# Attention and gated feed-forward in one kernel: PE transposes for the last 128 tokens of each chunk, pads of the second batch zeroed ahead of its DMA transposes, global rows doubled ahead

## The chip, the cores and the metric

One core of one Trainium2 chip runs the whole kernel. The metric is the device time of one execution in microseconds (us), lower is better. Before the change it is 449.09 us, the median of three runs (448.82 to 450.19).

The engines named below are PE (TensorE, matmuls; its weight loads are PEld), DVE (VectorE), ACT (ScalarE), POOL (GpSimd, which here also issues the loads) and SP (SyncE, which issues the DMA transposes and the stores). Each works through its own list of instructions in order, and semaphores hold one engine until another is done.

## What is computed

Attention with a window of 32 tokens and 8 global tokens over 8 batches x 8 heads x 576 tokens x 64 features, and behind it a gated feed-forward layer over all 4608 tokens (512 features, 1536 hidden):

```python
def _attn_ref(q, k, v, global_idx):
    scores = scale * np.matmul(q, k.transpose(0, 1, 3, 2))
    mask = np.abs(pos[:, None] - pos[None, :]) <= window
    mask = mask | is_global[:, None] | is_global[None, :]
    scores = np.where(mask, scores, -1000000000.0)
    scores = scores - np.max(scores, axis=-1, keepdims=True)
    attn = np.exp(scores)
    attn = attn / (np.sum(attn, axis=-1, keepdims=True) + 1e-09)
    return np.matmul(attn, v)

def _moe_ref(x, w_gate, w_val, w_out, w_res):
    g = x @ w_gate
    gelu = 0.5 * g * (1.0 + erf(g * inv_sqrt2))
    ffn_out = gelu * (x @ w_val) @ w_out
    res_gate = 1.0 / (1.0 + np.exp(-(x @ w_res)))
    return x + res_gate * ffn_out
```

x is the output of the attention, the heads of a token side by side. Matmuls run in bf16 with f32 sums.

## The kernel before, in words

**Chunks and batches.** The 4608 tokens are nine chunks of 512 (four tiles t = 0 to 3 of 128 tokens). A chunk is eight windows of 64 tokens, and a batch is nine windows, so chunk c uses batches c - 1 and c. The main loop (L491) runs over the chunks. While chunk c goes through the feed-forward layer, batch b = c + 1 is got ready and the attention of chunk c + 1 is computed, in between.

**First half of a chunk, ffn_in (L398).** Twelve rounds j, each of four matmuls into g_ps, four into v_ps, a Gelu on ACT (gsb) and a product on DVE (ht, L410). g_ps and v_ps take banks from psm, a pool of four PSUM banks that the other feed-forward results use too; ht gives v_ps's bank back. A second pool, pss (two banks, tag "sc"), holds the scores. Into these rounds the code puts the preparation of batch b: at the chunk's head turn_qk(b) (L295), ten DMA transposes issued by SP that write q and k of the batch with features on the partitions (qt, kt), and load_v(b); at j = 8 the shift of v, the load of the batch after it on POOL's queue, and prep_qz; at j = 11 the scores of the global tokens (sg, ss).

**Second half, ffn_out (L412).** Sixteen slots: for each tile a gate (r_ps, four matmuls) and three thirds of f_ps (twelve matmuls), with prb on DVE, ob on POOL and a store issued by SP at the end of the tile. Beside them stand the attention of the next chunk: scores in slots 0 to 7, values(t) in slot 5 + 2t (L351; its results are divided by DVE into xtok, L384), and turn_x(t) in slot 7 + 2t (L387), ahead of the slot's own work. turn_x writes xt, the chunk with features on the partitions, as ffn_in needs it. In chunk 0 it does so with four PE transposes into PSUM and a copy on ACT; in all later chunks with one DMA transpose that SP issues (L390). The last one, t = 3, stands in slot 13, ahead of the last twelve f_ps matmuls; the next chunk's first g_ps needs all four.

**Chunk 0 and batch 1.** The pads beside the data are written once for each of the two buffers. For batch 1 this stands in chunk 0: zero_qk(1) (L154, the halves of qz that stay zero and the pads of kt) behind round j = 0, zero_rest(1) (L160, ones and zeros in ve, pads of gt and ptg) behind j = 1, both on DVE. Ahead of the loop the loads of batch 1 (q, k, then v at L471) and of the weights (wr_t, wo_t) are put on POOL's queue, and behind them the gathers of the global rows of batches 2 to 7 (kgf, qgf, vgf, L191). turn_qk(1) stands at the head of chunk 0, ahead of zero_qk(1).

**Global rows.** spread_qk (L238) brings the gathered global rows of k and q into kgz and qgz: DVE doubles them in bf16 (kgd, qgd, L241), PE transposes them (tg, L245), DVE copies k's part and ACT q's (L250). It runs for the first pair of batches ahead of the loop (L457) and for the other three pairs in chunk 1 behind j = 6 (L512).

Of the kernel before, what the change touches and what calls it, by code (L numbers as in the profile page):

```python
# [9 lines left out]
BF16 = mybir.dt.bfloat16  # L10
# [6 lines left out]
def view(t, p0, pn, off, dims):  # L17

    step = t.ap[0][0]
    return bass.AP(tensor=t.tensor, offset=t.offset + p0 * step + off, ap=[[step, pn]] + dims)  # L20
# [3 lines left out]
def kernel(  # L24
# [12 lines left out]
    nc = tc.nc  # L37
    B, H, S, D = q.shape
# [14 lines left out]
    NKT = DM // 128  # L53
# [5 lines left out]
    pss = ctx.enter_context(tc.tile_pool(name="pss", bufs=2, space=bass.MemoryType.PSUM))  # L59
# [33 lines left out]
    def load_v(b):  # L93
        t = ve[b % 2]
        for c in range(5):
            p0, p1 = (32, 128) if c == 0 else (0, 96) if c == 4 else (0, 128)
            s0 = 128 * c - 32
            nc.gpsimd.dma_start(t[p0:p1, c, :, 0:D],  # L98
                                v[b].rearrange("h s d -> s h d")[s0 + p0:s0 + p1])
# [45 lines left out]
    def zero_wide(t, p0, pn, off, dims):  # L145

        w = [[st // 2, n] for st, n in dims[:-1]] + [[1, dims[-1][1] // 2]]
        b = t.bitcast(F32)
        nc.vector.memset(view(b, p0, pn, off // 2, w), 0.0)
# [4 lines left out]
    def zero_qk(i):  # L154
        for u in range(2):
            zero_wide(qz[i], 64 - 64 * u, 64, u * S, [[2 * S, NP], [1, S]])
        zero_wide(kt[i], 0, 128, 0, [[S + 64, NP], [1, 32]])
        zero_wide(kt[i], 0, 128, 32 + S, [[S + 64, NP], [1, 32]])
# [28 lines left out]
    gath = {what: const.tile([128, B // 2, D], F32, name=f"{what}gf", tag=f"{what}gf") for what in "kqv"}  # L187
# [41 lines left out]
    def hot_rows(i):  # L229
        r0 = 64 - 64 * (i % 2)  # L230
        nc.scalar.copy(gt[i][r0:r0 + 64, 64:64 + S], hot[r0:r0 + 64, :])


    twice = {what: const.tile([128, B // 2, 2, D], BF16, name=f"{what}gd", tag=f"{what}gd") for what in "kq"}
    vgb = const.tile([128, B // 2, VG], BF16, name="vgb", tag="vgb")
    nc.vector.memset(vgb[:, :, D:VG], 1.0)

    def spread_qk(n0, n1):  # L238
        nn = n1 - n0
        for what, big, pstep in (("k", kgz, 144), ("q", qgz, 16)):  # L240
            nc.vector.tensor_copy(twice[what][:, n0:n1, :, :],  # L241
                                  view(gath[what], 0, 128, n0 * D, [[D, nn], [0, 2], [1, D]]))
            tg = pss.tile([128, nn, 128], BF16, name="tg", tag="sc")
            for n in range(nn):
                nc.tensor.transpose(tg[:, n, :], twice[what][:, n0 + n, :, :].rearrange("p a d -> p (a d)"), ident)  # L245
            width = big.shape[2] * big.shape[3]
            for e in range(2):
                shift = 64 * e if what == "k" else 0
                for u in range(2):
                    (nc.scalar.copy if what == "q" else nc.vector.tensor_copy)(  # L250
                        view(big, 64 * u, 64, (2 * n0 + e) * width + shift + 8 * u,
                             [[2 * width, nn], [pstep, NP], [1, NG]]),
                        view(tg, 64 * u, 64, 64 * e + 8 * u, [[128, nn], [16, NP], [1, NG]]))
# [12 lines left out]
    def bank(shape, name, dt=F32):  # L266

        ring["n"] += 1
        if ring["n"] % 3 == 0:
            return pss.tile(shape, dt, name=name, tag="sc")  # L270
        return psm.tile(shape, dt, name=name, tag="mm")
# [23 lines left out]
    def turn_qk(b):  # L295
        for src, dst, c0 in ((q_st, qt[b % 2], 0), (k_st, kt[b % 2], 32)):
            for r in range(NQT):
                n = min(128, S - 128 * r)
                nc.sync.dma_start(dst[:, :, c0 + 128 * r:c0 + 128 * r + n], src[0:n, r, :], transpose=True)

    def prep_qz(b, p0, p1):
        for u in range(2):
            nc.vector.tensor_copy(qz[b % 2][64 * u:64 * u + 64, p0:p1, u, :],
                                  qt[b % 2][64 * u:64 * u + 64, p0:p1, :])
# [81 lines left out]

    def turn_x(c, t):  # L387
        mine = xt[c % 2][:, :, 128 * t:128 * t + 128]
        if c:
            nc.sync.dma_start(mine, xtok[c % 2][:, t, :], transpose=True)  # L390
            return
        tx = bank([128, NKT, 128], "tx", BF16)
        for kk in range(NKT):
            nc.tensor.transpose(tx[:, kk, :], xtok[c % 2][:, t, 128 * kk:128 * kk + 128], ident)
        nc.scalar.copy(mine, tx)


    def ffn_in(c, j):  # L398
# [45 lines left out]
    for p in range(NP + 1):  # L444
# [7 lines left out]
        if p:  # L452
            for what in "qk":
                turn_pair(p - 1, what, cast[what][1 if p < NP else 0])
            prep_qz(0, p - 1, p)
    hot_rows(0)
    spread_qk(0, 1)  # L457
    nc.vector.scalar_tensor_tensor(maskg, far, 1024.5, nong, ALU.is_gt, ALU.mult)
    shift_v(0)
# [31 lines left out]
    for c in range(NCH):  # L491
        b = c + 1
        if b < B:
            turn_qk(b)
            if b > 1:
                load_v(b)
        held = None
        for j in range(NFF):
            ffn_in(c, j)
            if b < B:  # L500
                if c == 0:
                    if j == 0:
                        zero_qk(1)
                    elif j == 1:
                        zero_rest(1, nc.vector)
                        hot_rows(1)
                    elif j == 2:
                        zero_globals(2, B)
                        spread_vg(1, nc.vector)
                if c == 1:  # L510
                    if j == 6:
                        spread_qk(1, B // 2)  # L512
                        spread_v(1, B // 2)
                    elif j == 8:
                        for n in range(2, B):
                            spread_vg(n, nc.gpsimd)
                if j == 8:
                    shift_v(b)
                    if b + 1 < B:
                        load_qk(b + 1)  # L520
                    prep_qz(b, 0, NP)
                if j == 11:
                    held = global_scores(b)
        slots = {n: [] for n in range(16)}
        if c + 1 < NCH:
            if held is not None:
                slots[0].append(lambda: global_exp(b, *held))
                slots[4].append(lambda: global_rows(b))
            for n in range(8):
                slots[n].append(lambda n=n: scores(c + 1, n // 4, n % 4))  # L530
            for t in range(4):
                slots[5 + 2 * t].append(lambda t=t: values(c + 1, t))
                slots[7 + 2 * t].insert(0, lambda t=t: turn_x(c + 1, t))
        work_f = [w for t in range(4) for w in ffn_out(c, t)]
        for n in range(16):
            for w in slots[n]:
                w()
            work_f[n]()
# [30 lines left out]
```

## Time and profile before

| | |
|---|---|
| median of three runs | 449.09 us (448.82, 449.09, 450.19) |
| the profiled execution | 448.51 us |
| its span, first to last instruction | 446.8 us |
| mean granted clock of PE | 0.975 |
| busy: PE / DVE / ACT / POOL | 87% / 46% / 38% / 37% |
| DMA moved | 47.60 MB, 107 GB/s over the span |
| xt by DMA transpose | 32 issues, median 2.4 us from issue to landing |
| qt and kt by DMA transpose | 35 each, median 7.1 and 5.2 us |

The profile is of one execution, with times from the span's start. A row of a timeline has start, duration, engine, line, operation, output <- input, shapes and a count; in square brackets stands the idle time of the engine just before it and what ended it. Equal instructions that follow each other make one row, whose duration runs from the first start to the last end. A row of the waits has the waiting engine and line, what it waited for, the total in us, how often, and the longest. A row of groups has the busy time, the mean of one in ns, and the idle time before. Some matmul records can be missing, so a group of four is sometimes shown as three.

### The profile page before, as it was taken

The page shows a single profiled execution, that of the slowest core. Times are in us where ns is not written, and L with a number is a line of the kernel's source. Part 1 is how long each engine was busy: PE and PEld are TensorE (multiplying, and loading weights), DVE is VectorE, ACT ScalarE, POOL GpSimd, SP SyncE. Part 2 cuts the span into 40 slices and gives each one's busy share as a digit, 9 for nine tenths or more (in the row PEclk, how much of TensorE's full clock was granted, in tenths as well). Part 3 has the DMA queues.
Part 4 walks back from the last instruction along what each step waited for, and adds up shares of the span by engine and source line. Part 5 has one row for each costly group of instructions (what it writes and reads, how often), then busy time and mean ns, then how long its engine had stood idle before and what let it go on. Part 6 is the DMA issues. An engine that isn't in the chain of part 4 may idle for free.

```text
span 446.8 us, 7136 instructions
## 1 busy us (share of the span) xinstructions
PE 387.6 (87%) x2718; PEld 207.3 (46%) x2762; DVE 204.5 (46%) x388; ACT 169.5 (38%) x274; POOL 167.2 (37%) x194
## 2 busy tenths in 40 slices
PE   2487049989799899989989998999899989998995
PEld 1373015644365346534644564456445644463442
DVE  6672055634555355435543553356344633462321
ACT  5364014523263236323623452345235423533320
POOL 6577346542672561257125613551420120022012
PEclk9999569999899999999999999999999999999999
DMA  7999997939393998399639973993592230022001
GB/s 173 168 168 156 167 209 108 126 94 152 70 114 76 138 175 84 83 129 182 62 96 126 172 77 82 151 173 50 100 148 67 37 106 2 0 73 70 0 23 72
DMA packets 168994, 47.60 MB, mean 107 GB/s; under 512 B 156480, under 2 KB 163136, under 8 KB 168960
## 3 DMA queue, kind: packets, MB, share of 16 engines
q0 software_dynamic: 108784, 18.62, 60.8%
q1 hardware_dynamic: 60176, 28.53, 32.2%
q8 instruction: 21, 0.34, 0.3%
q14 instruction: 13, 0.11, 0.1%
HBM read 39.19 MB, written 9.44 MB: 109 GB/s over the span
## 4 chain that ended last, share of the span: by engine, by line
PE 54%; issue 21%; DMA 13%; POOL 5%; DVE 3%; ACT 1%; SPq 1%; POOLq 0%; DVEq 0%
PE g_ps L402 15%; PE v_ps L406 14%; PE f_ps L429 11%; DMA wo_t<-in_moe_w_out_dram 4%; PE r_ps L419 4%; POOL ob L435 3%; DMA xt<-xtok 3%; DMA qt<-q_st 3%; PE sc L344 2%; PE nd L370 2%; DMA wo_t<-in_k_dram 2%; PE sg L310 2%; PE sn L332 1%; PE nd L364 1%; POOL k_st L90 1%
## 5 line engine op out<-in xcount | busy, mean ns | idle before, releaser
L406 PE MATMUL v_ps<-xt,wv_t 128*128 128x512 bf16 x417 | 110.3, 383 | 19.7 <-DVE ht L410 19.3
L410 DVE SCALAR_TENSOR_TENSOR ht<-gsb,v_ps 128x512 bf16<-128x512 bf16 x108 | 73.9, 687 | 112.7 <-PE v_ps L406 105.1
L409 ACT ACTIVATE gsb<-g_ps 128x512 bf16<-128x512 f32 x108 | 64.5, 597 | 158.3 <-PE g_ps L402 136.9
L402 PE MATMUL g_ps<-xt,wg_t 128*128 128x512 bf16 x429 | 112.1, 383 | 14.0 <-DMA xt<-xtok 12.9
L435 POOL TENSOR_TENSOR ob<-prb,xtok 128x512 f32<-128x512 f32 x36 | 41.9, 1163 | 204.0 <-DVE prb L433 201.7
L429 PE MATMUL f_ps<-wo_t,ht 128*128 128x512 bf16 x414 | 102.1, 379 | 0.9
L406 PEld LDWEIGHTS <-wv_t 128*128 128x128 bf16 x432 | 42.6, 99 | 71.5 <-issue 21.7
L402 PEld LDWEIGHTS <-wg_t 128*128 128x128 bf16 x432 | 42.0, 99 | 67.2 <-issue 13.3
L429 PEld LDWEIGHTS <-ht 128*128 128x128 bf16 x432 | 38.8, 98 | 35.9
L347 ACT ACTIVATE pt<-sc 128x512 bf16<-128x512 f32 x72 | 41.8, 598 | 28.4 <-PE sc L344 28.3
L422 ACT ACTIVATE rsb<-r_ps 128x512 bf16<-128x512 f32 x36 | 21.5, 596 | 61.8 <-PE r_ps L419 48.3
L349 DVE TENSOR_TENSOR pt<-pt,maskw 128x512 bf16<-128x512 bf16 x72 | 31.3, 437 | 27.1 <-ACT pt L347 25.6
L433 DVE SCALAR_TENSOR_TENSOR prb<-rsb,f_ps 128x512 f32<-128x512 bf16 x36 | 24.6, 684 | 33.4 <-PE f_ps L429 33.2
L90 POOL DMA_DIRECT2D q_st<-in_q_dram x35 | 30.0, 874 | 23.4 <-DMA qt<-q_st 23.4
L419 PE MATMUL r_ps<-wr_t,xt 128*128 128x512 bf16 x136 | 36.4, 379 | 0.4
L98 POOL DMA_DIRECT2D ve<-in_v_dram x40 | 34.3, 870 | 1.5 <-DMA k_st<-in_k_dram 1.5
L90 POOL DMA_DIRECT2D k_st<-in_k_dram x35 | 31.0, 912 | 6.6 <-DMA kt<-k_st 4.1
L344 PE MATMUL sc<-qz,kt 128*128 128x128 bf16 x288 | 27.8, 224 | 0.1
L344 PEld LDWEIGHTS <-kt 128*128 128x128 bf16 x288 | 21.8, 100 | 12.0
L384 DVE TENSOR_TENSOR xtok<-nd,rden 128x512 bf16<-128x512 f32 x34 | 23.5, 692 | 1.2
L370 PEld LDWEIGHTS <-pt 128*128 128x128 bf16 x576 | 22.3, 97 | 1.0
L370 PE MATMUL nd<-ve,pt 128*128 128x65 bf16 x320 | 22.3, 193 | 0.0
(103 smaller groups left out, 249.3 us busy)
## 6 DMA issues: line engine op xcount, KB each, us to landing
out_dram<-ob SPq DMA_DIRECT2D x36, 256.0 KB, 2.2
vo<-ve SPq DMA_DIRECT2D x16, 260.0 KB, 6.0
q_st<-in_q_dram POOLq DMA_DIRECT2D x28, 128.0 KB, 5.2
k_st<-in_k_dram POOLq DMA_DIRECT2D x28, 128.0 KB, 4.7
ve<-in_v_dram POOLq DMA_DIRECT2D x24, 128.0 KB, 5.5
ve<-in_v_dram POOLq DMA_DIRECT2D x16, 96.0 KB, 9.8
wg_t<-in_moe_w_gate_dram POOLq DMA_DIRECT2D x3, 512.0 KB, 6.1
wv_t<-in_moe_w_val_dram POOLq DMA_DIRECT2D x3, 512.0 KB
```

The lines of the kernel that those rows point to most:

```text
L90: nc.gpsimd.dma_start(dst[0:n, r, :].rearrange("p (h d) -> p h d", d=D), src[b].rearrange("h s d -> s h d")[128 * r:128 * r + n])
L98: nc.gpsimd.dma_start(t[p0:p1, c, :, 0:D], v[b].rearrange("h s d -> s h d")[s0 + p0:s0 + p1])
L344: nc.tensor.matmul(sc[:, n, :, :], kt[b % 2][:, p, 64 * i:64 * i + 128], qz[b % 2][:, p, :, 64 * i:64 * i + 64], start=True, stop=True)
L347: nc.scalar.activation(mine, sc, ACTF.Exp, bias=0.0, scale=SCALE)
L370: nc.tensor.matmul(nds[h // 4][:, VG * (h % 4):VG * (h % 4) + VG], view(pt, 0, 128, c0, [[1, 128]]), vw, start=False, stop=(h % 4 == 3 and ...
L402: nc.tensor.matmul(g_ps, wg_t[:, kk, 128 * j:128 * j + 128], x[:, kk, :], start=(kk == 0), stop=(kk == NKT - 1))
L406: nc.tensor.matmul(v_ps, wv_t[:, kk, 128 * j:128 * j + 128], x[:, kk, :], start=(kk == 0), stop=(kk == NKT - 1))
L409: nc.scalar.activation(gsb, g_ps, ACTF.Gelu, bias=0.0, scale=1.0)
L410: nc.vector.scalar_tensor_tensor(ht[:, j, :], gsb, 0.5, v_ps, ALU.mult, ALU.mult)
L419: nc.tensor.matmul(r_ps, xt[c % 2][:, kk, 128 * t:128 * t + 128], wr_t[:, kk, :], start=(kk == 0), stop=(kk == NKT - 1))
L429: nc.tensor.matmul(held["f"], ht[:, j, 128 * t:128 * t + 128], wo_t[:, j, :], start=(j == 0), stop=(j == NFF - 1))
L435: nc.gpsimd.tensor_tensor(ob, prb, xtok[c % 2][:, t, :], ALU.add)
```

## The change

turn_x for t = 3 of chunks 1 to 8 goes back to four PE transposes, into a bank of pss, with the copy to xt on DVE; t = 0 to 2 stay DMA transposes. zero_qk(1) stands at the head of chunk 0, ahead of turn_qk(1). The doubling is taken out of spread_qk into a function of its own: for the first pair both casts stand ahead of the transposes, for the other three pairs they stand in chunk 1 behind j = 3. zero_rest(1) keeps its place.

```diff
+    def double_qk(n0, n1):
+        for what in "kq":
+            nc.vector.tensor_copy(twice[what][:, n0:n1, :, :],
+                                  view(gath[what], 0, 128, n0 * D, [[D, n1 - n0], [0, 2], [1, D]]))
+
     def spread_qk(n0, n1):
         nn = n1 - n0
         for what, big, pstep in (("k", kgz, 144), ("q", qgz, 16)):
-            nc.vector.tensor_copy(twice[what][:, n0:n1, :, :],
-                                  view(gath[what], 0, 128, n0 * D, [[D, nn], [0, 2], [1, D]]))
             tg = pss.tile([128, nn, 128], BF16, name="tg", tag="sc")
...
     def turn_x(c, t):
         mine = xt[c % 2][:, :, 128 * t:128 * t + 128]
-        if c:
+        if c and t < 3:
             nc.sync.dma_start(mine, xtok[c % 2][:, t, :], transpose=True)
             return
-        tx = bank([128, NKT, 128], "tx", BF16)
+        tx = pss.tile([128, NKT, 128], BF16, name="tx", tag="sc") if c else bank([128, NKT, 128], "tx", BF16)
         for kk in range(NKT):
             nc.tensor.transpose(tx[:, kk, :], xtok[c % 2][:, t, 128 * kk:128 * kk + 128], ident)
-        nc.scalar.copy(mine, tx)
+        (nc.vector.tensor_copy if c else nc.scalar.copy)(mine, tx)
...
     hot_rows(0)
+    double_qk(0, 1)
     spread_qk(0, 1)
...
         if b < B:
+            if c == 0:
+                zero_qk(1)
             turn_qk(b)
...
                 if c == 0:
-                    if j == 0:
-                        zero_qk(1)
-                    elif j == 1:
+                    if j == 1:
                         zero_rest(1, nc.vector)
                         hot_rows(1)
...
                 if c == 1:
-                    if j == 6:
+                    if j == 3:
+                        double_qk(1, B // 2)
+                    elif j == 6:
                         spread_qk(1, B // 2)
```

The places where instructions move, in the order of the built program (line numbers behind the first edit are three higher in the changed kernel).

DVE at the start of chunk 0, before (qz_77 and kt_79 are batch 1's buffers, ve_81 its v):

```order
L410 SCALAR_TENSOR_TENSOR ht<-gsb,v_ps 128x512
L149 MEMSET qz_77 64x4x288 x2
L149 MEMSET kt_79 128x4x16 x2
L410 SCALAR_TENSOR_TENSOR ht<-gsb,v_ps 128x512
L161 MEMSET ve_81 128x40
L162 MEMSET ve_81 32x520
```

The same place in the changed kernel:

```order
L149 MEMSET qz_77 64x4x288 x2
L149 MEMSET kt_79 128x4x16 x2
L413 SCALAR_TENSOR_TENSOR ht<-gsb,v_ps 128x512 x2
L161 MEMSET ve_81 128x40
L162 MEMSET ve_81 32x520
```

The memsets of qz and kt have moved ahead of the product of round 0; those of ve stand behind round 1 as before.

PE between the gate of tile 3 and the last f_ps of chunk 0, before (xt_88 is this chunk's xt, xtok_91 the next chunk's tokens):

```order
L419 LDWEIGHTS xt_88
L419 MATMUL r_ps<-wr_t,xt_88 128x512
L429 LDWEIGHTS ht
L429 MATMUL f_ps<-wo_t,ht 128x512
L429 LDWEIGHTS ht
```

The same place in the changed kernel:

```order
L422 LDWEIGHTS xt_88
L422 MATMUL r_ps<-wr_t,xt_88 128x512
L397 LDWEIGHTS xtok_91
L397 MATMUL tx<-ident,xtok_91 128x128
L397 LDWEIGHTS xtok_91
L397 MATMUL tx<-ident,xtok_91 128x128
L397 LDWEIGHTS xtok_91
L397 MATMUL tx<-ident,xtok_91 128x128
L397 LDWEIGHTS xtok_91
L397 MATMUL tx<-ident,xtok_91 128x128
L432 LDWEIGHTS ht
L432 MATMUL f_ps<-wo_t,ht 128x512
```

Four transposes now stand between the gate and f_ps, at this place in chunks 0 to 7.

DVE in chunk 1 around rounds 3 to 8, before (kgd and qgd are the doubled rows):

```order
L410 SCALAR_TENSOR_TENSOR ht<-gsb,v_ps 128x512 x7
L241 CAST kgd<-kgf 128x384
L250 COPY kgz<-tg 64x3x4x8 x4
L241 CAST qgd<-qgf 128x384
L256 CAST vgb<-vgf 128x3x64
L410 SCALAR_TENSOR_TENSOR ht<-gsb,v_ps 128x512 x2
```

The same place in the changed kernel:

```order
L398 COPY xt_89<-tx 128x4x128
L436 SCALAR_TENSOR_TENSOR prb<-rsb,f_ps 128x512
L413 SCALAR_TENSOR_TENSOR ht<-gsb,v_ps 128x512 x4
L240 CAST kgd<-kgf 128x384
L240 CAST qgd<-qgf 128x384
L413 SCALAR_TENSOR_TENSOR ht<-gsb,v_ps 128x512 x3
L253 COPY kgz<-tg 64x3x4x8 x4
L259 CAST vgb<-vgf 128x3x64
L413 SCALAR_TENSOR_TENSOR ht<-gsb,v_ps 128x512 x2
```

Both casts have moved three rounds forward, and the copy of the new transposes stands between the last two prb of the chunk before.

## The prediction

> **What bounds the kernel now.** I read the page first (busy times and the 40 slices), then the list of waits, then timelines of single engines at the places that the waits name. The page has PE as the busiest engine, and its row of 40 slices shows where it is not; the row under it is the clock granted to it:
>
> ```profile
> PE   2487049989799899989989998999899989998995
> PEclk9999569999899999999999999999999999999999
> ```
>
> Past the start, its only empty slices are the fifth and the sixth (11.2 us each, 45 to 67 us); later it is at 8 or more. There the clock falls to 5 and 6 tenths. So time is gained only where PE itself stands idle, and the list of waits says on what (columns: total us, times, longest):
>
> ```profile
> PE v_ps L406 <- DVE ht L410: 19.3, 2, 17.7
> PE g_ps L402 <- DMA xt<-xtok: 12.9, 8, 1.7
> ```
>
> The 12.9 us are eight waits, one at the head of each of chunks 1 to 8. The 19.3 us stand in chunk 0 and go back to VectorE (DVE), which itself waits at the pads of kt (Part 4). A third place, in chunk 1, is shown in Part 2. The change aims at all three.
>
> **Part 1, the last 128 tokens of a chunk.** The first of the eight heads, on PE, on DVE, which makes the tokens, and on SP:
>
> ```profile
> 94.56 2.75 PE L429 MATMUL f_ps<-wo_t,ht 128*128 128x512 bf16 x12
> 98.98 1.02 PE L402 MATMUL g_ps<-xt,wg_t 128*128 128x512 bf16 x4 [1.66 <-DMA xt<-xtok]
> ...
> 93.03 0.21 DVE L383 RECIPROCAL rden<-nd 128x8 f32<-128x8 f32 x1 [1.50 <-PE nd L370]
> 93.28 0.69 DVE L384 TENSOR_TENSOR xtok<-nd,rden 128x512 bf16<-128x512 f32 x1
> 94.00 0.69 DVE L433 SCALAR_TENSOR_TENSOR prb<-rsb,f_ps 128x512 f32<-128x512 bf16 x1
> ...
> 91.66 2.56 SPq L390 DMA_TRANSPOSE xt<-xtok  x2
> 96.37 1.23 SPq L390 DMA_TRANSPOSE xt<-xtok  x1
> ```
>
> The order on PE is gate, twelve f_ps matmuls, next chunk's g_ps. Twelve take 2.75 us, of which the last alone 0.38 (the mean of one in the groups of lines, below), so one starts every (2.75 - 0.38)/11 = 0.216 us, and the next instruction could start 12 x 0.216 = 2.59 us after 94.56, at 97.15; it starts at 98.98. This head costs 1.83 us. For all eight, from the row of the waits: 12.9, plus eight times the 0.38 - 0.22 = 0.16 by which a matmul's end trails the next one's possible start, together 14.2 us. The end of it is the DMA transpose that SP issues at 96.37.
>
> The change takes that DMA away and puts four PE transposes between gate and f_ps, and one DVE copy out of PSUM. The price on PE is in chunk 0, where the same transposes run today:
>
> ```profile
> L429 PE MATMUL f_ps<-wo_t,ht 128*128 128x512 bf16 x414 | 102.1, 379 | 0.9
> 29.38 0.40 PE L394 MATMUL tx<-ident,xtok 128*128 128x128 bf16 x4
> 29.61 0.39 PE L364 MATMUL nd<-vgs,gt 128*128 128x260 bf16 x2
> L394 PE MATMUL tx<-ident,xtok 128*128 128x128 bf16 x16 | 1.9, 223 | 1.0 <-DVE xtok L378 1.0
> ```
>
> Four of them hold PE from 29.38 to 29.61, 0.23 us. They need xtok, which DVE ends at 93.28 + 0.69 = 93.97; the transposes come up at 94.56, 0.59 us later, so no wait. The copy stands on DVE behind prb at 94.00, which ends at 94.69; DVE's other op from PSUM to 128x512 bf16, xtok's, took 0.69, so I estimate the copy from 94.95 to 95.6, while g_ps would start at 97.15 + 0.23 = 97.4: hidden, with 1.8 us to spare; if that cover went, it would cost 0.7 per head. The next to land is the transpose of the third quarter, the second of the two that SP issues from 91.66 to 94.22; the last one is done at most 98.98 - 96.37 = 2.6 us from its issue, so this one by 96.8: also before 97.4. On SP the output stores no longer stand on either side of a transpose; POOL keeps its order. Sum: 8 x 0.23 = 1.8 added, 14.2 gone, **-12.4 us**.
>
> The Trainium skill, page "TensorE: Matmul & The Clock Gate", Part 4, speaks against this price: a 128x128 bf16 PE transpose took about 275 ns in a kernel, and needs a copy out of PSUM. By that figure 32 transposes are 8.8 us and the sum here would be -5.4. This trace has 0.23 us for four in a row, so the measurement decides.
>
> **Part 2, the doubling in chunk 1.** PE and DVE at that place:
>
> ```profile
> 109.33 1.03 PE L402 MATMUL g_ps<-xt,wg_t 128*128 128x512 bf16 x4
> ...
> 112.54 0.34 PE L245 MATMUL tg<-ident,kgd 128*128 128x128 bf16 x3 [1.53 <-DVE kgd L241]
> 114.42 0.50 PE L245 MATMUL tg<-ident,qgd 128*128 128x128 bf16 x3 [1.54 <-DVE qgd L241]
> 114.72 1.91 PE L402 MATMUL g_ps<-xt,wg_t 128*128 128x512 bf16 x4
> ...
> 117.86 1.03 PE L402 MATMUL g_ps<-xt,wg_t 128*128 128x512 bf16 x4
> ...
> 111.33 0.69 DVE L410 SCALAR_TENSOR_TENSOR ht<-gsb,v_ps 128x512 bf16<-128x512 bf16 x1 [1.04 <-PE g_ps L402]
> 111.94 0.55 DVE L241 CAST kgd<-kgf 128x384 bf16<-128x384 f32 x1
> ```
>
> PE stands through both DVE casts (1.53 us for k, 1.54 for q), and then runs slow for one round (g_ps 1.91 for four where 1.03 is usual). One round of g_ps and v_ps is 2 x 0.863 = 1.73 us; from 109.33 without the stop, the round after next (117.86) would start at 109.33 + 2 x 1.73 = 112.79, plus six transposes at 0.057 = 0.34: 113.13. Saved: **-4.7 us**. The two casts move to j = 3, where DVE has 1.04 us free in a round (the idle time in the row of 111.33); they need 1.10, if q's takes as long as k's 0.55, so ht is 0.06 late there and catches up in the next round; four PSUM banks between PE and DVE cover it. Should the cover fail, it is 0.1. The rows they read were requested long before:
>
> ```profile
> 71.91 1.33 POOL L191 DMA_INDIRECT qgf<-in_q_dram,idx  x1 [2.56 <-DMA wo_t<-in_moe_w_out_dram]
> DMA to landing us min/median/max: 7.9/13.1/18.2
> ```
>
> The last of those for the casts leaves at 71.91 and lands by 90.1 even with the longest of kgf's landings, 14 us before j = 3 (about 104).
>
> **Part 3, the start.** The first doubling now casts q before the k copies; it can save at most the 0.38 + 0.23 us of these rows, and I take 0, for what follows waits for loads (Part 4) and swallows it.
>
> ```profile
> 18.94 0.73 DVE L250 COPY kgz<-tg 64x32 bf16<-64x32 bf16 x4 [0.38 <-PE tg L245]
> 19.70 0.23 DVE L241 CAST qgd<-qgf 128x128 bf16<-128x128 f32 x1
> ```
>
> **Part 4, the pads of batch 1.** This is the largest wait, and I give it nothing. DVE, then PE, in chunk 0:
>
> ```profile
> 36.28 0.69 DVE L410 SCALAR_TENSOR_TENSOR ht<-gsb,v_ps 128x512 bf16<-128x512 bf16 x1 [3.00 <-PE v_ps L406]
> ...
> 38.56 1.02 DVE L149 MEMSET qz<- 64x1152 f32 x1 [0.28 <-issue]
> 59.08 0.19 DVE L149 MEMSET kt<- 128x64 f32 x2 [19.51 <-DMA kt<-k_st]
> ...
> 60.83 0.09 DVE L161 MEMSET ve<- 128x40 bf16 x1 [0.97 <-DMA ve<-in_v_dram]
> ...
> 62.48 0.63 DVE L410 SCALAR_TENSOR_TENSOR ht<-gsb,v_ps 128x512 bf16<-128x512 bf16 x1
> ...
> 59.91 1.86 PE L406 MATMUL v_ps<-xt,wv_t 128*128 128x512 bf16 x4 [17.68 <-DVE ht L410]
> ...
> 63.16 1.02 PE L406 MATMUL v_ps<-xt,wv_t 128*128 128x512 bf16 x4
> ...
> 66.41 1.02 PE L406 MATMUL v_ps<-xt,wv_t 128*128 128x512 bf16 x4 [1.57 <-DVE ht L410]
> ...
> 79.78 1.03 PE L429 MATMUL f_ps<-wo_t,ht 128*128 128x512 bf16 x4
> ...
> 51.70 19.95 DMA wo_t<-in_moe_w_out_dram
> ```
>
> Today DVE waits 19.5 us for the kt transposes, does ht of j = 1 and then waits another 0.97 us, to 60.83, at the next pads (L161, zero_rest), for the v loads of batch 1. That second wait isn't touched. With the kt pads early, DVE does ht of j = 1 near 38 and stands at L161 instead until the same 60.83, with every later ht queued behind it. PE does one round more (the v_ps of 59.91 today and the g_ps behind it) and then needs the PSUM bank that ht of j = 2 frees at 62.48 + 0.63 = 63.1: the v_ps of 63.16 starts at 63.16 again. The round that PE is ahead is spent on the clock: the first two groups after the stop take 63.16 - 59.91 = 3.25 us today in place of 1.73, and after the change it is the groups of 63.16 and 64.02 that run slow, to 63.16 + 3.25 = 66.41, just when ht of j = 3 frees the next bank. So 0, at most about 1.6 lost if the slow clock lasts for one round more. The early memsets are two of 1.02 with 0.28 of issue each, and 0.19: 2.8 us, in a place where DVE idles 3.00 for the first v_ps (row of 36.28). Without that cover PE would have four banks of slack before it notices, so 0 again.
>
> **The sum.** -12.4 - 4.7 = -17.1. The profiled execution took 448.5 us (span 446.8), the median is 449.09: 0.6 more. 448.5 - 17.1 + 0.6 = **432.0 us**, some 3.8% faster. About 0.3% (1.35 us) is what a measurement here can tell from no change.
>
> **Rivals.**
> (a) *The next batch's transposes become late.* They follow the last output store on SP, which follows f_ps, now 0.23 later, while PE enters the chunk 1.6 earlier: 1.8 us less margin. In chunk 2:
>
> ```profile
> L315 PE MATMUL ss<-qgz,kt x20: 169/169/173, 169.3 to 169.7; 128*128 128x16 bf16 x20
> L299 SPq DMA_TRANSPOSE kt<-k_st x5: 1199/1216/2598, 155.3 to 161.9; - x5
> DMA to landing us min/median/max: 4.4/4.9/7.0
> ```
>
> The last kt piece leaves at 161.9 and lands 4.4 to 7.0 later, 166.3 to 168.9; its reader comes by 169.7. The margin of 0.8 to 3.4 loses 1.8: 0 to 1.0 us. At 1.0 in this chunk and, as an estimate, a third of it in six others, 434.8; at 1.0 in all seven, 439. Chance 0.11.
> (b) *PE transposes take their full time.* If each held PE for the row's mean of 223 ns, 32 would cost 7.1 in place of 1.8: 437.3. Against it: 0.23 for four at 29.38. Chance 0.05. It is the rule of the Trainium skill's Part 4, named above, taken as this kernel's rows would have it.
> (c) *The wait for the v loads does not hold.* Then PE goes on until f_ps needs wo_t, landed at 51.70 + 19.95 = 71.65: up to 79.78 - 71.65 = 8.1 more, 423.9. Against it: the 0.97 us of wait at 60.83 today, after kt was done. Chance 0.05.
> (d) *Slower: PE is held at its own transposes.* Today a late xtok holds only SP; now it holds f_ps behind it on PE, in order. It decides from 0.59 us late, and eats 17.1 + 1.35 us when each head waits 2.3, so when xtok ends 2.9 us later than now, at 96.9; at 3.5 later the time is 432.0 + 8 x 2.9 = 455. Against it: DVE idles 1.5 us ahead of that rden. Chance 0.02; 0.02 more for a lateness that leaves the time within 0.3%.
> (e) *The change doesn't do what it says*: the order of the changed program has every move in it, so nothing is kept for this.
>
> **The numbers.** The forecast has 0.75, with its own range of 430.4 (Part 3 and 1 us for what else was missed) to 433.6 (the slow clock). (a), (b) and (c) are faster too: faster 0.96, same 0.02, slower 0.02. The range takes in the forecast, (a) up to 436.5 and the bounds of Part 3: 429.5 to 436.5; (b), (c), (d) and the end of (a) stay out, under 0.2.
>
> **What would show it.** Right: no wait of g_ps for xtok in the list, and g_ps 2.6 us after the first of the twelve f_ps; g_ps of chunk 1 in rounds of 1.73 through j = 7; DVE's wait at L161 near 21 us in place of 19.5 + 0.97, and v_ps again near 63.2. Wrong: v_ps of chunk 0 well before 60, a wait of PE for tx or xtok, ss waiting for kt, or a chunk period other than about 1.5 us shorter.

## The result, and the profile after

| | before | after |
|---|---|---|
| median of four runs each, on one chip | 449.64 us (448.82 to 451.55) | 433.85 us (433.35 to 434.48) |
| ratio, after to before | | 0.9644, 95% interval 0.9609 to 0.9679 |
| the profiled execution, span | 448.51, 446.8 us | 433.35, 431.6 us |
| busy PE / DVE | 87% / 46% | 90% / 49% |
| xt by DMA transpose | 32 issues | 24 issues |

Faster by 3.6%, inside the range of the prediction; from profile to profile 15.2 us are gone where 17.1 were forecast. First the 40 slices of the profile after, PE and its granted clock:

```profile
PE   2578009999999999999999999999999999999995
PEclk9999758999999999999999999999999999999999
```

Behind the start PE is now at nine tenths or more in every slice but the fifth and the sixth, which are empty, and the last, in which the kernel ends. The stop in chunk 0 is still there; the clock is at 7 and 5 in it and at 8 in the slice behind it. The timeline of PE at the first chunk head (columns as before: start, duration, engine, line, operation, count):

```profile
95.14 1.03 PE L422 MATMUL r_ps<-wr_t,xt 128*128 128x512 bf16 x4
96.01 0.39 PE L397 MATMUL tx<-ident,xtok 128*128 128x128 bf16 x4
96.23 2.75 PE L432 MATMUL f_ps<-wo_t,ht 128*128 128x512 bf16 x12
98.82 1.03 PE L405 MATMUL g_ps<-xt,wg_t 128*128 128x512 bf16 x3
```

The four transposes hold PE from 96.01 to 96.23, and g_ps starts 98.82 - 96.23 = 2.59 us after the first of the twelve f_ps, with no idle time in brackets. The wait for xtok's DMA is gone from all eight heads: from 72 us on PE never stands for longer than 0.14 us. DVE's copy out of PSUM and the two doublings in chunk 1, on DVE, and the transposes of the doubled rows, on PE:

```profile
96.43 0.42 DVE L398 COPY xt<-tx 128x512 bf16<-128x512 bf16 x1 [0.30 <-PE tx L397]
106.60 0.55 DVE L240 CAST kgd<-kgf 128x384 bf16<-128x384 f32 x1
107.06 0.55 DVE L240 CAST qgd<-qgf 128x384 bf16<-128x384 f32 x1
107.72 0.69 DVE L413 SCALAR_TENSOR_TENSOR ht<-gsb,v_ps 128x512 bf16<-128x512 bf16 x1
115.57 2.98 DVE L306 COPY qz<-qt 64x2304 bf16<-64x2304 bf16 x2
```
```profile
110.04 1.03 PE L409 MATMUL v_ps<-xt,wv_t 128*128 128x512 bf16 x4
110.91 0.33 PE L248 MATMUL tg<-ident,kgd 128*128 128x128 bf16 x3
111.07 0.33 PE L248 MATMUL tg<-ident,qgd 128*128 128x128 bf16 x3
```

Where PE stood twice for 1.5 us there is no stop; the casts and the ht behind them follow each other without a gap that PE sees. The row of 115.57 is used further down. Last, chunk 0, DVE and then PE:

```profile
35.89 0.18 DVE L149 MEMSET kt<- 128x64 f32 x2
61.88 0.09 DVE L161 MEMSET ve<- 128x40 bf16 x1 [23.14 <-DMA ve<-in_v_dram]
```
```profile
64.21 1.87 PE L409 MATMUL v_ps<-xt,wv_t 128*128 128x512 bf16 x4 [20.22 <-DVE ht L413]
65.87 1.49 PE L405 MATMUL g_ps<-xt,wg_t 128*128 128x512 bf16 x3
67.58 1.29 PE L409 MATMUL v_ps<-xt,wv_t 128*128 128x512 bf16 x4 [0.22 <-DVE ht L413]
77.34 1.14 PE L313 MATMUL sg<-qt,kgz 128*128 128x288 bf16 x8
```

The pads of kt are done at 36 us in place of 59, and DVE then stands at the next memset, that of ve, for 23.1 us, until the v loads have landed. One long wait has taken the place of two. It ends at 61.88, before at 60.83.

The length of a chunk, from its first g_ps to the next chunk's, from the timelines of PE (the ninth, about 40.0 us in both, has no next head):

| chunk | 0 | 1 | 2 | 3 | 4 | 5 | 6 | 7 |
|---|---|---|---|---|---|---|---|---|
| before | 64.68 | 48.57 | 43.80 | 43.43 | 43.81 | 43.43 | 43.81 | 40.96 |
| after | 64.48 | 42.88 | 42.19 | 41.98 | 42.19 | 41.97 | 42.19 | 39.38 |
| gone | 0.20 | 5.69 | 1.61 | 1.45 | 1.62 | 1.46 | 1.62 | 1.58 |

Forecast were 12.4 / 8 = 1.55 us for a head in the mean (1.83 - 0.23 = 1.60 for the first), and 4.7 more in chunk 1. So chunks 2 to 7 are as forecast, about 0.6 us is missing in chunk 1 (6.25 forecast, 5.69 gone), and in chunk 0 1.4 of the 1.6 of its head. The experiments look for these two, and try the prices of the parts one by one.

### The profile page after: what moved, and what is told of

It reads as the page before. It is cut to its first block, busy times and chain, and to the rows that moved or that the text cites. A ratio compares the mean times of both kernels' runs of the same rounds, so it can differ in the third digit from the quotient of the medians.

```text
span 431.6 us, 7189 instructions
## 1 busy us (share of the span) xinstructions
PE 386.6 (90%) x2749; PEld 208.9 (48%) x2794; DVE 209.6 (49%) x396; ACT 169.6 (39%) x274; POOL 167.9 (39%) x194
## 4 chain that ended last, share of the span: by engine, by line
PE 74%; issue 8%; POOL 1%; DVE 1%; POOLq 0%; DVEq 0%
PE f_ps L432 19%; PE v_ps L409 18%; PE g_ps L405 17%; PE r_ps L422 6%; PE nd L373 4%; PE sc L347 3%; PE nd L367 2%; PE sn L335 2%; PE sg L313 2%; POOL ob L438 1%; PE ss L318 1%; DVE qz L306 1%; PE tx L397 0%; POOLq L570 0%; DVE ht L413 0%
## 5 line engine op out<-in xcount | busy, mean ns | idle before, releaser
L409 PE MATMUL v_ps<-xt,wv_t 128*128 128x512 bf16 x431 | 111.8, 382 | 21.0 <-DVE ht L413 20.4
L405 PE MATMUL g_ps<-xt,wg_t 128*128 128x512 bf16 x415 | 109.4, 381 | 1.1 <-ACT xt L398 0.7
## 6 DMA issues: line engine op xcount, KB each, us to landing
wv_t<-in_moe_w_val_dram POOLq DMA_DIRECT2D x3, 512.0 KB, 12.7
```

Source lines behind the costliest of these rows:

```text
L405: nc.tensor.matmul(g_ps, wg_t[:, kk, 128 * j:128 * j + 128], x[:, kk, :], start=(kk == 0), stop=(kk == NKT - 1))
L409: nc.tensor.matmul(v_ps, wv_t[:, kk, 128 * j:128 * j + 128], x[:, kk, :], start=(kk == 0), stop=(kk == NKT - 1))
```

## The experiments

e1 to e4 share a chip and its runs of the kernel before (448.75 us), e5 to e8 another (448.79), e9 to e12 a third (450.32). The kernel before itself thus moves by 1.6 us between these sets, and each ratio is to the runs of its own set.

**e1, the pads back behind j = 0** (an edit of the changed kernel):

```diff
-            if c == 0:
-                zero_qk(1)
             turn_qk(b)
...
-                    if j == 1:
+                    if j == 0:
+                        zero_qk(1)
+                    elif j == 1:
```

> The changed kernel with the pads of batch 1 zeroed behind j=0 again, as before the change; all else stays. Theory T (the pads' move buys and costs nothing, since VectorE stands at the memset of ve until the v loads have landed in either order): within 0.5 us of the changed kernel's 433.85, chunk 0 still 64.5 us from g_ps to g_ps. Rival R1 (the move itself is what made the v loads land later and took back the 1.4 us that chunk 0 lacks): 432.3 to 432.8, VectorE past the ve memset near 60.8 instead of 61.9, chunk 0 near 63.1 us.

Measured: 433.43 us, ratio 0.9658 (0.963 to 0.9686), the same as the change within its interval. In the profile chunk 0 took 64.68 us and the ve memset came at 62.65, later than with the move, not sooner. That goes against R1's reason, though the row of sg below has more on it. DVE and PE of this kernel:

```profile
60.60 0.18 DVE L149 MEMSET kt<- 128x64 f32 x2 [20.81 <-DMA kt<-k_st]
62.65 0.09 DVE L161 MEMSET ve<- 128x40 bf16 x1 [1.27 <-DMA ve<-in_v_dram]
```
```profile
61.42 1.86 PE L409 MATMUL v_ps<-xt,wv_t 128*128 128x512 bf16 x4 [18.99 <-DVE ht L413]
77.72 1.14 PE L313 MATMUL sg<-qt,kgz 128*128 128x288 bf16 x8
```

PE resumes at 61.42, 1.2 us ahead of the landing of v, and from the ve memset to the first sg matmul there are 77.72 - 62.65 = 15.07 us; in the changed kernel 77.34 - 61.88 = 15.46. Before, the first sg matmul stands here:

```profile
75.90 1.14 PE L310 MATMUL sg<-qt,kgz 128*128 128x288 bf16 x8
```

That is 75.90 - 60.83 = 15.07 us again. Two separate things thus make up the 1.4 us of chunk 0: 1.05 us of landing and 0.39 behind it.

**e2, the PE transposes alone** (the kernel before with only the edit of turn_x):

```diff
-        if c:
+        if c and t < 3:
...
-        tx = bank([128, NKT, 128], "tx", BF16)
+        tx = pss.tile([128, NKT, 128], BF16, name="tx", tag="sc") if c else bank([128, NKT, 128], "tx", BF16)
...
-        nc.scalar.copy(mine, tx)
+        (nc.vector.tensor_copy if c else nc.scalar.copy)(mine, tx)
```

> The kernel before with the PE transposes of the last 128 tokens as the only edit. Theory T: 449.64 minus eight heads at 1.45 to 1.62 us (12.4) is 437.2; chunk 0 near 63.1 us, because its head is one of the eight and the v loads are not touched. Rival R2 (what chunk 0 lacks belongs to this edit): chunk 0 near 64.5 and 438.6. Rival R3 (transposes at some 0.22 us each rather than 0.22 us for four): about 442.

Measured: 437.96 us, ratio 0.9749 (0.9716 to 0.9782), that is 9.8 to 12.7 us less than before; T's 12.4 is in it, R3's 7 is not. Chunks 2 to 7 took 42.20, 41.97, 42.20, 41.97, 42.19 and 39.38 us, those of the changed kernel to 0.01. Chunk 0 took 64.39 us, which is R2's number but not for R2's reason: the head did its part, and v landed late, at 62.44, although nothing in this kernel touches the loads. From the sg matmul (77.51) to the next head it took 21.48 us, as in the changed kernel (98.82 - 77.34 = 21.48) and against 98.98 - 75.90 = 23.08 before: 1.60 us gone at the head of chunk 0, as forecast.

**e3, the two doublings alone** (the kernel before with double_qk, called ahead of spread_qk(0, 1) and at j = 3 of chunk 1):

```diff
+    double_qk(0, 1)
     spread_qk(0, 1)
...
-                    if j == 6:
+                    if j == 3:
+                        double_qk(1, B // 2)
+                    elif j == 6:
```

> The kernel before with both doublings ahead as the only edit. Theory T: chunk 1 loses the stop at the transposes of the doubled rows, 4.1 to 4.7 us, and the first doubling gives nothing: 444.9 to 445.5, the ve memset near 60.8 as before. Rival R4 (the first doubling starts the loads 0.8 us sooner, they then collide with more traffic and v lands about 1 us later): ve memset near 61.9, chunk 0 near 66, 446.0 to 446.9.

Measured: 445.55 us, ratio 0.993 (0.9906 to 0.9955), 2.0 to 4.2 us less. Chunk 1 took 44.42, 4.15 less than in the first profile of before: T's lower end. v landed at 62.97, chunk 0 took 67.33 us. That is R4's sign, and with e1 (62.65) it would make the early loads suspect; but e2 landed v at 62.44 without them.

**e4, the pads' move alone** (an edit of the kernel before):

```diff
+            if c == 0:
+                zero_qk(1)
             turn_qk(b)
...
-                    if j == 0:
-                        zero_qk(1)
-                    elif j == 1:
+                    if j == 1:
```

> The kernel before with the pads of batch 1 zeroed ahead of its DMA transposes as the only edit. Theory T: 449.64 within 0.5, ve memset near 60.8. Rival R1 (the move costs): 450.6 to 451.0, ve memset near 61.9, chunk 0 near 66 us.

Measured: 451.45 us, ratio 1.0062 (1.0038 to 1.0087): 1.7 to 3.9 us slower, more than either theory gave. v landed at 62.19. PE of this kernel, and its stretches of two us (columns: stretch, its length, busy us and count of PE, PEld, DVE, ACT and POOL, PE's granted clock, DMA share, GB/s):

```profile
64.52 1.87 PE L406 MATMUL v_ps<-xt,wv_t 128*128 128x512 bf16 x4 [20.59 <-DVE ht L410]
78.63 1.14 PE L310 MATMUL sg<-qt,kgz 128*128 128x288 bf16 x8
```
```profile
64.00:66.00 2.00, 1.48 (x4) 0.56 (x4) 1.73 (x2) 0.60 (x1) 0.85 (x1) 0.50 1.25 208
66.00:68.00 2.00, 2.00 (x6) 0.72 (x5) 1.96 (x5) 0.00 (x0) 0.00 (x0) 0.50 1.13 291
68.00:70.00 2.00, 2.00 (x6) 0.65 (x5) 1.01 (x3) 0.60 (x1) 0.12 (x1) 0.50 1.17 207
70.00:72.00 2.00, 2.00 (x10) 0.90 (x9) 0.58 (x2) 0.60 (x1) 0.82 (x1) 0.90 1.21 250
```

From the ve memset to sg it took 78.63 - 62.19 = 16.44 us, 1.37 more than with the pads behind j = 0. PE ran at half its clock until the stretch of 70 to 72, whose mean of 0.90 puts the step to full speed at 70 + 2 x (1 - 0.90) / 0.5 = 70.40, 5.9 us after PE had resumed. The same stretches of e1:

```profile
60.00:62.00 2.00, 0.58 (x2) 0.25 (x2) 0.77 (x3) 0.54 (x1) 0.95 (x1) 0.50 1.38 167
62.00:64.00 2.00, 2.00 (x7) 0.65 (x5) 1.04 (x3) 0.06 (x1) 1.69 (x2) 0.50 1.24 205
64.00:66.00 2.00, 2.00 (x6) 0.63 (x5) 1.68 (x6) 0.60 (x1) 1.14 (x2) 0.50 1.24 207
66.00:68.00 2.00, 1.49 (x6) 0.52 (x5) 1.96 (x4) 0.00 (x0) 0.00 (x0) 0.93 1.18 285
```

By the same working (0.93 in the last row) the half clock lasts to 66.28, 4.9 us, but it begins 1.2 us before v has landed, and PE has a round in hand: it costs nothing that sg would see.

**e10, e11 and e12, the kernel before and e4 once more**, unchanged (no diff).

> The kernel before, word for word, once more. Theory T (the v loads land anywhere between 60.8 and 63.0 us from run to run; the first trace of before, at 60.83, was an early one, and the four kernels with the pads where before has them, three of them at 62.4 to 63.0, are the rule): VectorE past the ve memset at 61.5 to 63, from there 15.07 us to the first sg matmul as in the first trace, chunk 0 at 65.3 to 67 us. Rival R9 (the kernel before lands v at 60.8 each time, and each of the edits delays it): 60.8 again, chunk 0 at 64.7. Ratio to before 1 within 0.3%.

> The kernel before a third time, for one more sample of the time at which the v loads land: T 61.5 to 63, R9 60.8.

> The pads' move alone a second time. Theory T2 (the move lets PE stand without a break until v lands, so that its half clock is paid behind the landing; how much depends on when the clock comes back): from the ve memset to the first sg matmul 15.3 to 16.5 us, against 15.07 with the pads behind j=0; PE at clock 0.5 for 3 to 6 us after it resumes. Rival (the 16.44 us of the first look were chance): 15.1.

Measured: e10 450.04 us, ratio 0.999 (0.9971 to 1.0008); e11 448.22 and e12 450.46 us, one run each. e10, DVE and PE:

```profile
59.69 0.19 DVE L149 MEMSET kt<- 128x64 f32 x2 [20.09 <-DMA kt<-k_st]
62.18 0.09 DVE L161 MEMSET ve<- 128x40 bf16 x1 [1.72 <-DMA ve<-in_v_dram]
```
```profile
60.52 1.86 PE L406 MATMUL v_ps<-xt,wv_t 128*128 128x512 bf16 x4 [18.27 <-DVE ht L410]
77.25 1.14 PE L310 MATMUL sg<-qt,kgz 128*128 128x288 bf16 x8
```

T is confirmed against R9: v landed at 62.18 in e10 and at 62.05 in e11, and chunk 0 took 66.00 and 65.85 us. The first profile of before, at 60.83, was an early draw. e12 alone would speak against T2: 15.11 us from the ve memset (62.78) to sg, the rival's number. But all twelve profiles that hold this wait side by side, with the time for which PE runs at half clock after it has resumed (worked out as under e4), bring T2 out:

| pads behind j = 0 | ve memset | to sg | | pads ahead | ve memset | to sg | half clock |
|---|---|---|---|---|---|---|---|
| before | 60.83 | 15.07 | | e12 | 62.78 | 15.11 | 3.17 |
| e10 | 62.18 | 15.07 | | e8 | 62.05 | 15.32 | 3.62 |
| e11 | 62.05 | 15.07 | | after | 61.88 | 15.46 | 3.91 |
| e1 | 62.65 | 15.07 | | e6 | 62.23 | 15.64 | 4.24 |
| e2 | 62.44 | 15.07 | | e7 | 62.23 | 15.72 | 4.44 |
| e3 | 62.97 | 15.06 | | e4 | 62.19 | 16.44 | 5.88 |

The landing shows no clear order by the edits (the two latest, e3 and e12, share none). The way from it to sg does. With the pads behind it is the same to 0.01 us, whatever the clock: the half clock lasts 3.1, 3.6, 6.0, 4.8, 5.3 and 5.2 us there (in the order of the table), but it begins ahead of the landing, and full speed is back 2.0 to 4.6 us after the ve memset. With the pads ahead it is back 5.5 to 8.2 us after it. There the way grows with the half clock, in all six by 0.5 x (half clock - 3.1): 0.04, 0.26, 0.41, 0.57, 0.67 and 1.39 by this, 0.04, 0.25, 0.39, 0.57, 0.65 and 1.37 measured against 15.07. So some 3.1 us of half clock are covered by the round that PE is ahead, and of each us beyond it half is lost.

e11 shows one thing more, in chunk 1. PE's stretches of two us in e10, and then in e11:

```profile
114.00:116.00 2.00, 0.46 (x6) 0.29 (x5) 1.64 (x6) 0.00 (x0) 0.00 (x0) 0.84 0.19 37
116.00:118.00 2.00, 2.00 (x8) 0.82 (x6) 0.00 (x0) 0.93 (x4) 1.87 (x2) 0.50 0.97 241
```
```profile
114.00:116.00 2.00, 0.46 (x6) 0.28 (x5) 1.64 (x6) 0.01 (x1) 0.10 (x1) 1.00 0.19 37
116.00:118.00 2.00, 2.00 (x11) 0.94 (x10) 0.22 (x1) 1.52 (x5) 1.93 (x2) 1.00 0.95 243
```

The two stops at the doubled rows are the same, 1.53 and 1.54 us; but in e11 the clock stays at 1.00 behind them, and chunk 1 takes 47.04 us where e10 takes 48.49. About 1.45 of the 4.7 us of Part 2 are thus slow clock, which not every execution has. The traces' own records of the granted clock show what decides it. In all fourteen profiles the clock changes only on a grid of 3.41 us (in the first profile of before the half clock of chunk 0 runs from 45.90 to 62.97 us, 17.07 = 5 x 3.413), and the grid lies elsewhere in each execution. In e10 both stops fall mainly into one stretch of it, 111.93 to 115.35, in which PE stands for 2.65 us, and the next stretch is at half. In e11 the grid cuts between them, PE stands for 1.87 and 1.20 us, and the clock stays. The other four profiles with both stops (before, e2, e4, e12) have 2.0 to 2.9 us of them in one stretch, and the next one is at half.

**e6 and e7, more tiles by PE transposes** (the changed kernel, e6 with two tiles as shown, e7 with all four: there the branch with the DMA transpose is gone):

```diff
-        if c and t < 3:
+        if c and t < 2:
```

> The changed kernel with the third 128 tokens of a chunk by PE transposes too. Theory T (four transposes cost PE 0.22 to 0.23 us, and the DMA transpose that they replace was hidden): eight more groups, 1.8 us more, 435.6. Rival R3 (each transpose costs PE some 0.22 us): 7 us more, 441. Rival R6 (the shorter SyncE queue lets the stores or the next batch's transposes start sooner, and something waits for these): no change or a gain.

> The changed kernel with all tokens by PE transposes. Theory T: three more groups per chunk, 24 in all at 0.22 to 0.23 us, 5.4 us more: 439.2. Rival R3: 21 us more, 455. Rival R6: less than T, 434 to 437. If it comes out above T but far below R3, the sc buffers that the transposes now share with the scores, or VectorE's copies, have become a wait; the trace then shows PE idle ahead of tx or sc.

Measured: e6 436.03 us, ratio 0.9707 (0.967 to 0.9743), e7 439.36 us, 0.977 (0.9729 to 0.9811). PE of e6 ahead of chunk 2:

```profile
137.19 0.39 PE L397 MATMUL tx<-ident,xtok 128*128 128x128 bf16 x4
137.42 0.39 PE L367 MATMUL nd<-vgs,gt 128*128 128x260 bf16 x2
```

Each group holds PE for 0.22 to 0.23 us. Chunks 2 to 7 take 0.22 to 0.23 us more than after the change in e6 (42.42 against 42.19, 42.20 against 41.98), and 0.67 in e7 (42.86, 42.65) for three groups: T to the hundredth, R3 and R6 fall. With all tiles on PE, Part 1 would have gained 12.4 - 5.4 = 7.0 us, since three of a chunk's four DMA transposes were hidden.

**e8, the global rows' spread at j = 3** (the changed kernel):

```diff
                     if j == 3:
                         double_qk(1, B // 2)
+                        spread_v(1, B // 2)
+                        for n in range(2, B):
+                            spread_vg(n, nc.gpsimd)
...
                         spread_qk(1, B // 2)
-                        spread_v(1, B // 2)
-                    elif j == 8:
-                        for n in range(2, B):
-                            spread_vg(n, nc.gpsimd)
```

> The changed kernel with the copies of the global rows of batches 2 to 7 (vgb on VectorE, vgs on GpSimd) started at j=3 of chunk 1 instead of j=6 and j=8, so that GpSimd's six tensor_tensors no longer run beside VectorE's qz copies. Theory T (a VectorE copy that runs beside GpSimd's takes longer: 2.98 us for two qz copies here, 2.17 us in the next chunk): qz copies of chunk 1 at 2.2 us or less, v_ps of j=11 0.3 us sooner, 433.5. Rival R7 (the qz copies take what they take, whatever GpSimd does): 2.98 us again and 433.85.

Measured: 432.72 us (429.87 to 434.35), ratio 0.9629 (0.9586 to 0.9671): too close to the change for its runs to tell. The profile does tell. POOL and DVE after the change:

```profile
113.11 7.47 POOL L263 TENSOR_TENSOR vgs<-vgb,diag 64x520 bf16<-64x520 bf16 x6 [7.89 <-DVE vgb L259]
129.04 1.15 POOL L438 TENSOR_TENSOR ob<-prb,xtok 128x512 f32<-128x512 f32 x1
```
```profile
129.53 0.94 DVE L352 TENSOR_TENSOR pt<-pt,maskw 128x512 bf16<-128x512 bf16 x1 [0.93 <-ACT pt L350]
```

and in e8:

```profile
109.10 5.54 POOL L263 TENSOR_TENSOR vgs<-vgb,diag 64x520 bf16<-64x520 bf16 x5
126.89 1.15 POOL L438 TENSOR_TENSOR ob<-prb,xtok 128x512 f32<-128x512 f32 x1 [3.27 <-DVE prb L436]
```
```profile
115.59 1.78 DVE L306 COPY qz<-qt 64x2304 bf16<-64x2304 bf16 x2
129.24 0.43 DVE L352 TENSOR_TENSOR pt<-pt,maskw 128x512 bf16<-128x512 bf16 x1 [0.92 <-ACT pt L350]
```

With POOL out of the way the two qz copies take 1.78 us in place of 2.98, and chunk 1 takes 42.31 us in place of 42.88. The cast vgb, which the edit moves too, plays no part in that: the copies start at 115.57 and at 115.59. Chunk 1 gains 0.57, more than the 0.3 of T. Of it 0.31 stand ahead of the first sg (21.36 us from the head after the change, 21.05 in e8), as T has it; the other 0.26 is the row of 129.53. With POOL late, its ob product comes at 129.04 beside DVE's product of pt, which takes 0.94 in place of 0.43 and holds the tokens behind it; in e8 ob is done before. R7 falls.

**e5, the memsets of batch 1 ahead of the v loads** (the changed kernel; all six memsets of zero_rest go to a place where DVE idles for 2.5 us):

```diff
+    zero_rest(1, nc.vector)
     shift_v(0)
...
                     if j == 1:
-                        zero_rest(1, nc.vector)
                         hot_rows(1)
```

> The changed kernel with the six memsets of batch 1's ve, gt and ptg moved from behind j=1 of chunk 0 to the place behind maskg, where VectorE is idle for 2.5 us, ahead of the v loads, so that they no longer wait for v. Theory T (VectorE's wait for the v loads, 23.1 us, is the bound of chunk 0, and what comes next is the landing of the second batch's DMA transposes and of wo_t's second half near 73 us, against its first use at about 81): PE's 20.2 us stop at the third pair goes, a part comes back in front of the qz copies at j=8 and at the second third of f_ps, and 6 to 10 us are left: 424 to 428. Rival R5 (the whole of the loads, not one landing, bounds chunk 0, so that the wait only moves to the next thing loaded): 432 to 434. Of the question where 1.4 us went in chunk 0 it says whether the time at which v lands sets the end of chunk 0.

Measured: 426.29 us (425.07 to 427.0), ratio 0.9487 (0.9455 to 0.9519), 7.0 us below the change by the two ratios and 7.6 by the two medians. Chunk 0 takes 58.12 us. PE of e5 where it still waits:

```profile
49.17 1.04 PE L405 MATMUL g_ps<-xt,wg_t 128*128 128x512 bf16 x4 [0.97 <-DMA wg_t<-in_moe_w_gate_dram]
51.98 1.04 PE L409 MATMUL v_ps<-xt,wv_t 128*128 128x512 bf16 x4 [1.78 <-DMA wv_t<-in_moe_w_val_dram]
60.48 0.26 PE L318 MATMUL ss<-qgz,kt 128*128 128x16 bf16 x4 [0.88 <-DMA kt<-k_st]
62.93 1.04 PE L422 MATMUL r_ps<-wr_t,xt 128*128 128x512 bf16 x3 [1.95 <-DMA wr_t<-in_moe_w_res_dram]
68.51 1.89 PE L432 MATMUL f_ps<-wo_t,ht 128*128 128x512 bf16 x4 [4.32 <-DMA wo_t<-in_moe_w_out_dram]
72.61 1.01 PE L432 MATMUL f_ps<-wo_t,ht 128*128 128x512 bf16 x2 [0.93 <-DMA wo_t<-in_moe_w_out_dram]
```

The 20 us stop is gone, and PE now meets the loads one by one: wg_t (0.97), wv_t (1.78), kt (0.88), wr_t (1.95), wo_t (4.32 and 0.93). T holds: the landing of v did bound chunk 0, because DVE stood at ve with every later ht behind it, and what comes next is wo_t. The qz copies at j = 8, which T had as a second wait, cost nothing. The clock is still lost: it is at half from 64.26 to 77.91 us by its records, in and behind the waits for wr_t and wo_t.

**e9, the edits of e5 and of e8 together** (both diffs as above).

> The changed kernel with two of the earlier edits together: batch 1's memsets ahead of the v loads (alone 426.29) and the global rows' spread at j=3 (its chunk 1 was 0.57 us shorter). Theory T (they act in different chunks and add): 425.7, chunk 0 at 58.1 us, chunk 1 at 42.3. Rival R8 (with chunk 0 shorter, chunk 1 meets GpSimd's queue while the loads still run, so that the spread starts no sooner): 426.3.

Measured: 426.58 us (425.7 to 427.48), ratio 0.9472 (0.9449 to 0.9496). Chunk 1 took 42.31 us, so the 0.57 of e8 are there; chunk 0 took 59.51, for the loads came later: PE's first wait for wo_t ended at 69.61 against 68.51 in e5. In the end it is e5's time. Both beat the change; between the two nothing is decided.

## Why the prediction was right, and where it was off

**Part 1 was right, as a mechanism and in size.** 12.4 us were forecast. Measured are 9.34 in chunks 2 to 7, 1.60 in chunk 0 (from sg to the next head), and in chunk 1 the 1.40 that e2 has against the first profile of before (48.57 - 47.17): 12.3. The two prices on which it rests were both taken from rows of this kernel, 0.23 for four transposes and 2.59 for twelve f_ps. e6 and e7 doubled and quadrupled the first and found 0.22 to 0.23 each time. The Trainium skill, page "TensorE: Matmul & The Clock Gate", Part 4, has about 275 ns for one such transpose. That is the duration of one, for which the rows of before have a mean of 223 ns; the sum needs the time for which PE is held, and the runs show that where four follow each other one holds it for 0.22 / 4 = 0.06 us. Only the copy was off: 0.42 us for an estimate of 0.67, off the path either way.

**Part 2 was right in the stop and missed who stands beside it.** Where 4.7 us were forecast, 4.15 came in alone (e3) and 4.29 on top of the transposes (e2's 47.17 to 42.88); with e8's edit, which takes POOL's products away, it is 4.86 (47.17 to 42.31). The failed step is the list of what is late next: an edit which brings the qz copies forward, from 120.47 to 115.57, brings them wholly under POOL's six products (113.11 to 120.58); the forecast went through PE and DVE for it and left out POOL. Before, only the last of these products, which ended at 121.38, stood beside them:

```profile
120.47 2.57 DVE L303 COPY qz<-qt 64x2304 bf16<-64x2304 bf16 x2
```

They took 2.57 us there and 2.98 after. Of the 4.7 about 1.5 were slow clock behind the stops, which e11 did not have.

**Part 3 was right.** The first doubling brought sg of batch 0 forward (19.34 us after 20.07), and the start of chunk 0 came at 34.34 us against 34.30: swallowed by the loads. Over all profiles it came at 34.27 to 34.60 without the doubling ahead and at 33.78 to 34.51 with it, so that a few tenths in some executions can't be told apart from none.

**Part 4 is the term that was mis-sized**, and within its bound. "So 0, at most about 1.6 lost if the slow clock lasts for one round more": it was 0.39 in the profile of the change, 0.04 to 1.37 over six profiles, 0.55 in the mean. The wait moved from kt to ve as forecast, and its end isn't set by the pads. The step that failed is "the round that PE is ahead is spent on the clock": that takes the half clock for about as long as in the one profile it was read from, where PE resumed at 59.91 and the stretch of 62 to 64 us has a clock of 0.76, so 3.1 us. Just so much is covered, and e12, with 3.17, paid next to nothing; but the half clock lasted up to 5.9. The profile of the forecast had the shortest of all twelve, and that was bad luck. With the pads behind j = 0 PE resumes at 59.9 to 61.7, ahead of v, and warms up while DVE still waits; with the pads ahead it resumes at 64.2 to 65.1, behind v, and pays. The Trainium skill, "TensorE: Matmul & The Clock Gate", Part 1, says that full speed returns after a busy window of about 3.4 us, and that the windows run freely. By that rule the half clock would last, as an estimate, between one window and two, 3.4 to 6.8 us; the twelve profiles here have 3.1 to 6.0, so the spread agrees and the lower end is a little lower. The records of the clock show how that comes. At half clock, a stretch of the 3.41 us grid in which PE stood for 0.42 us or less was followed by full speed, and one with 0.84 us or more was not, in all fourteen profiles. In before PE resumed 0.36 us behind the start of a stretch, which still counted, so the half clock ended with it; in e4 it resumed 0.94 us behind the start of one, and the half clock lasted to the end of the next. Against the start of the span the grid lies anywhere, 0.02 to 3.41 us in the fourteen profiles.

The sign that was named for this part, DVE's wait at L161 near 21 us, came as 23.14. The rows of the forecast themselves give about 22 (from the end of ht of j = 1, near 38.7, to 60.83), and the late landing is the rest.

**The rest of chunk 0 was no effect at all.** 1.05 of the missing us are the landing of v, 60.83 in the profile on which the forecast was made and 61.9 to 63.0 in all eleven others, two of the same kernel among them. Why it spreads wasn't found: neither the early loads nor the pads set it.

**The rivals.** (a) did not come: no wait of ss for kt is in the list. Its time was also added up wrong: 1.0 and a third of it in six others are 3.0, which gives 435.0 and not 434.8. (b) is excluded by e6 and e7. (c), that the wait for v doesn't hold, did not come with this change, for DVE stood at ve for 23.1 us; e5 is the edit that brings it, with 426.29 us where (c) gave 423.9. (d) did not come; the transposes found xtok ready (no idle time at 96.01).

Put together, from profile to profile: 12.3 (Part 1) + 4.7 (Part 2) - 0.6 (POOL beside DVE) - 0.4 (slow clock) - 1.05 (landing) = 14.95, measured 15.2.

What stays open: whether the pads' move is worth keeping in the changed kernel (e1 and the change can't be told apart; alone it cost 1.7 to 3.9 us by e4's runs and nothing to 1.4 by the profiles; why the six runs of e4 lie that far from those of before on their chip isn't known), and whether e5 needs it. Its kt pads would have had to wait for the transposes to about 60 us otherwise; that was argued, not run.

## What to carry to other kernels

A long wait of an in-order engine is seldom one wait: before moving what it waits at, look which instruction behind it waits for a landing about as late, and move that one (e5's six memsets were worth 7 us, the group that the change moved nothing). When a step is brought forward, ask on the shared paths, not only on the queues, what it will now run beside. And a forecast that leans on one profiled landing should carry the spread of a second profile of the same kernel.

## What the runs showed of the hardware that was not expected

**VectorE beside GpSimd.** A 128x512 bf16 product on DVE took 0.94 us beside POOL's ob product (129.04 to 130.19) and 0.43 otherwise. It ended at 130.47, 0.28 after POOL's. The other products of pt in this profile that began beside a running product of POOL and were held by it ended 0.29 us after POOL's too: 1.14 us from 24.45, 0.57 us from 85.35. The two qz copies took 2.98 us beside POOL's products in the changed kernel, each ending 0.61 to 0.62 us after one of them, and 1.78 in e8 beside POOL's DMA issues. Begun first, DVE isn't held: from 378.35 it took 0.43 us, and POOL's ob from 378.36 took 1.43 in place of 1.15. The Trainium skill, "SBUF — State Buffer", section "SBUF: two separate sides", says that the two engines share a pair of ports as an exclusive lock, and that the later one blocks until the other's instruction ends. The traces agree: in these rows the one that began later was held. That the product ended 0.28 us behind POOL's, and not its whole 0.43, leaves some 0.15 us of it that passed beside POOL's, as an estimate.

**The clock moves on a grid of 3.41 us** that lies elsewhere in each execution, so the half clock after a stop lasts unequally: 3.1 to 6.0 us after stops of 17.7 to 20.9 us, and after two stops of 1.5 us it came in e10 and stayed away in e11. **Landings spread**: the same v loads, issued in the same order, landed between 60.83 and 62.18 us in three profiles of one kernel.
